# Two attention blocks on one core: the maxima's rows without TensorE, two projection groups moved into the loop, and one order for all loop steps

## The chip, the cores and the metric

The kernel runs on one core of a Trainium2 chip. The metric is the device time of one execution in microseconds (us). Before the change the median of 3 runs is 1849.92 us (1848.37 to 1851.09).

Five engines work side by side, each through its own instructions in program order: TensorE (PE, with its weight loads PEld), VectorE (DVE), ScalarE (ACT), GpSimd (POOL) and the DMA queue of SyncE (SP). They wait for each other through semaphores.

## The reference

Two attention blocks on 2048 rows of width 640, 32 heads of 20 columns each, both in float32. Block A is a dilated sliding window (8 keys per row), block B is full attention:

```python
q, k, v = x @ wqkv                       # per head 2048 x 20
scores = einsum("bhqd,bhkd->bhqk", q, k) * 20 ** -0.5
o = einsum("bhqk,bhkd->bhqd", softmax(scores), v)
out = o @ wo                             # A and B side by side
```

## The kernel before, in words

**Projections (0 to 442 us).** First Q, K and V of block A, then Q and K of block B, then V of block B. V of block B is made in 32 groups of 128 rows by 320 columns (lines 758 to 791): 15 matmuls into one of the four small PSUM banks `ps_st`, a copy by ScalarE into a tile `ve`, and a store to `vb_d` in DRAM one tick later.

**Block B, the loop (442 to 1805 us).** 8 head groups of 4 heads, 4 query blocks (`qc`) of 512 rows each, 16 key blocks of 128 rows each: 8 x 4 x 16 = 512 steps, numbered `i`, and 32 *units* of 16 steps (a unit is one head group and one query block). A step has three parts:

- `b_qk(i)`: the transposed scores of the step, 2 pairs of matmuls (the two of a pair work on different halves of the rows of the array), and 4 exponentials by ScalarE into tiles `e`.
- `b_pv(i - 2)`: the product with V, two steps later (`LAG`), 4 matmuls in the program and 8 in the trace. `hold` says over how many steps it is summed in PSUM: 2, so that ScalarE copies (`more`) and GpSimd adds (`braw`) once in two steps. Units 27 to 29 (`ALONE`) have `hold` 1.
- `b_max(i + 24)`: the plain scores of a step 24 later (`LEAD`), 2 pairs of matmuls into one of two wide PSUM tiles `ps_mx` each, and for each a maximum over 512 keys by VectorE (`mx<-ps_mx`). The softmax needs the row maximum before its exponential, so the maxima run 24 steps ahead of it.

**Maxima's rows.** At the end of a unit's 16 maxima, `max_rows` (line 560) makes one number per query of them and hands it to the score matmuls as two more rows of the tile `bq` (one rounded, one with the rest), against rows of -1 in `bk`. VectorE reduces `m4` to `m1` (128 x 16, `mx<-mx`); two ticks later `turn` is put into the list `rows`, which the loop takes up in its odd steps: TensorE transposes `m1` into a PSUM bank (`ps_st<-ident,mx`), ScalarE copies 16 x 128 of it (`mtr`), VectorE subtracts the copy from the bank for the rest, the bank is given back; one tick later one DMA stores 16 x 2 x 128 to `mdr` in DRAM, and one more tick later two DMAs load the rows into `bq` (`bq<-mdr`). In the loop, for unit u, the reduction comes at step 16u-7, the transpose at 16u-5, the store at 16u-4, the load at 16u-3; the unit's first score matmul is in step 16u.

**Steps 432 to 479** (units 27 to 29) go through `b_both` (line 632) in place of `b_qk` and `b_max`: score matmuls and maxima's matmuls alternate one by one, on opposite halves of the array, and the product with V comes last.

**The V groups and the maxima.** The first 24 steps of `b_max` have to come before the loop; one of them follows each V group from the 9th to the 32nd (`groups > 8`, line 780). The Q rows that they need are loaded after the first four V groups, four DMAs each.

**Other work in the loop.** Block A's attention is GpSimd's (`akv`, `al`, `ao`); its output projection comes as pieces of 15 matmuls (`ps_st<-ww,aot`) in some steps. The sum of the exponentials comes back through DRAM as a tile `sm`, of which VectorE takes the reciprocal (`sm<-sm`). `after(n, ...)` puts an instruction n ticks (steps) later; its engine's own order is the order in which these calls run. All transfers named here go through SP's queue, in order; each waits until the one eight places before it has landed.

Of the kernel before, what the change touches and what calls it, by code (L numbers as in the profile page):

```python
# [8 lines left out]
F32 = mybir.dt.float32  # L9
# [8 lines left out]
DH = 20  # L18
# [24 lines left out]
ALONE = range(27, 30)  # L43
# [16 lines left out]
def attention_pair(ctx, tc, xa, wqk_a, wv_a, wo_a, xb, wqk_b, wv_b, wo_b, oa, ob):  # L60
# [497 lines left out]
    rows = []  # L558
# [48 lines left out]
    mxt = {}  # L607

    def b_max(i):
# [4 lines left out]
        if sub == 0:  # L614
            mxt[u] = (sb.tile([128, 2, 8, 4], F32, tag="mx4", bufs=2, name="mx4"),
                      sb.tile([128, 16], F32, tag="mx1", bufs=2, name="mx1"))
# [14 lines left out]

    def b_both(i):

        u, kb = divmod(i, NKB)
        g, qc = divmod(u, NQC)
        q, k, v = stacks[g]
        P[i] = []
        i1 = i + LEAD
        u1, sub = divmod(i1, NKB)
        g1, qc1 = divmod(u1, NQC)  # L640
        q1, k1, _ = stacks[g1]
        if sub == 0:
            mxt[u1] = (sb.tile([128, 2, 8, 4], F32, tag="mx4", bufs=2, name="mx4"),
                       sb.tile([128, 16], F32, tag="mx1", bufs=2, name="mx1"))
        m4, m1 = mxt[u1]
        pq, ch = divmod(sub, 2)
        pl1, qb = divmod(pq, 4)
        for pl in range(2):
            e = sb.tile([128, 2, 512], F32, tag="p", bufs=PB, name="e")
            c = 2 * ch + pl  # L650
            w = wide()
            for r in range(2):
                rows = slice(r * HALF, r * HALF + BM)
                p = bank()
                pe.matmul(p, k[rows, pl, kb * 128:kb * 128 + 128], q[rows, qc, pl], start=True, stop=True)
                act.activation(e[:, r], p, AF.Exp, scale=SCALE)
                give(p)
                rows = slice((1 - r) * HALF, (1 - r) * HALF + BS)
                pe.matmul(w[:, 1 - r], q1[rows, qc1, pl1, qb * 128:qb * 128 + 128],
                          k1[rows, pl1, c * 512:(c + 1) * 512], start=True, stop=True)  # L660
            dve.tensor_reduce(m4[:, :, pq, c], w, AX.X, ALU.max)
            P[i].append(e)
        if sub == NKB - 1:
            max_rows(m4, m1, q1, qc1)
# [26 lines left out]
    def b_pv(i):  # L691
        u, kb = divmod(i, NKB)
        g, qc = divmod(u, NQC)
        hold = 1 if u in ALONE else 2
        n, part = divmod(kb, hold)
# [3 lines left out]
        for j in range(GH):  # L699
            pe.matmul(acc[32 * j:32 * j + 32, :], stacks[g][2][:, kb, j * VC:j * VC + 32], P[i][j % 2][:, j // 2],  # L700
                      start=(part == 0), stop=(part == hold - 1))
        del P[i]
        if part < hold - 1:
            return
# [53 lines left out]
    for n in (2, 3, 0, 1):  # L758
        for half in range(2):
            for s in range(4 * n, 4 * n + 4):  # L760
                p = bank()
                rows15(p, lambda xi, k: chunk(XB[n], xi, k)[:, s % 4 * 128:s % 4 * 128 + 128], WV[half])
                ve = ones[s % 4]
                act.copy(ve[:, :16 * VC].rearrange("p (h c) -> p h c", c=VC)[:, :, :DH],
                         p[:, :320].rearrange("p (h d) -> p h d", d=DH))
                give(p)
                c = 16 * VC + 11 * half
                after(1, sp.dma_start, vb_d[s * 128:(s + 1) * 128, half * 16 * VC:half * 16 * VC + c], ve[:, :c])
                tick()
                groups += 1  # L770
                if q_loads:
                    for _ in range(4):
                        q_loads.pop(0)()
                if groups == 1:
                    wait[0] = 5
                if groups in (8, 16):
                    XB[groups // 8 - 1], more = x_pieces(xb, groups // 8 - 1, gp)
                    for fn in more:
                        fn()
                if groups > 8:  # L780
                    for i in islice(steps, 1):
                        for _ in b_max(i):
                            pass
                    if rows:
                        rows.pop(0)()
                if groups > 16 and groups % 3 == 0 and groups != 21:
                    next(a_work, None)
                if groups in (26, 28):
                    v_piece(0, *((0, 4) if groups == 26 else (8, 16)))
# [4 lines left out]
    for h in range(2):  # L794
        w, more = wide_pieces(wo_a[h], gp)
        WO.append(w)
        loads += more
    assert next(steps, None) is None

    spare += [sb.tile([128, 2, 512], F32, tag="last0", bufs=2, name="more") for _ in range(2)]
# [14 lines left out]
    for i in range(NS + LAG):  # L817
# [16 lines left out]
        if i // NKB in ALONE and i + LEAD < NS:  # L834
            b_both(i)
            if rows and i % 2:
                rows.pop(0)()
            b_pv(i - LAG)
            if fill and i % 2 == 0:
                fill.pop(0)()  # L840
            elif i % 6 == 4 and not out_piece() and not left_a[0] and not WO_b:
                for h in range(2):
                    w, more = wide_pieces(wo_b[h], gp)
                    WO_b.append(w)
                    loads += more
            continue
        if i + LEAD >= NS:
# [3 lines left out]
            if rows and i % 2:  # L851
                rows.pop(0)()
# [8 lines left out]
        if rows and i % 2:  # L861
            rows.pop(0)()
        if i >= LAG:
            b_pv(i - LAG)
        next(qk, None)
        mx = b_max(i + LEAD)
        next(mx, None)
        if fill and i % 2 == 0:
            fill.pop(0)()
        elif i % 6 == 4 and not out_piece() and not left_a[0] and not WO_b:  # L870
            for h in range(2):
                w, more = wide_pieces(wo_b[h], gp)
                WO_b.append(w)
                loads += more
# [58 lines left out]
```

## Time and profile before

| | us |
|---|---|
| median of 3 runs | 1849.92 |
| the profiled execution's own time | 1849.53 |
| its span in the trace | 1847.8 |
| PE busy (matmuls) | 1805.9 (98%) |
| ScalarE busy | 1363.9 (74%) |
| VectorE busy | 1320.7 (71%) |
| GpSimd busy | 1233.1 (67%) |
| first score matmul of step 0 | 442.24 |
| first score matmul of step 432 / 480 | 1586.28 / 1710.36 |

The matmuls' ends are modelled and overlap, so a PE busy at 98% is not a PE at its limit. The times of steps are taken from the timeline: a step begins with its first score matmul (`ps_st<-bq,bk`). A row of the windows view has the stretch (us from the span's start), its length, then for PE, PEld, DVE, ACT and POOL the busy time and number of instructions, the granted clock of TensorE (1.00 is full), the DMA share and GB/s.

### The profile page before, as it was taken

Reading aid. Unit: us, or ns where it says so; the run is one execution under the profiler, and the core shown is the slowest. Engines: PE = TensorE matmul, PEld = TensorE weight load, DVE = VectorE, ACT = ScalarE, POOL = GpSimd, SP = SyncE. Lnnn points to the kernel's source line nnn. Section 1 sums busy time; section 2 is a strip of 40 time slices with the busy share of each in tenths; the row PEclk is TensorE's granted clock in tenths of the full one; section 3 lists DMA queues with packets and bytes.
Section 4 is the critical chain, followed back from the end, with each engine's and each line's share of the span. In section 5 each row is a group of like instructions: output and inputs, shape, how many; then the busy total and the mean of one; then the engine's idle time right before and its main releaser. Section 6 shows DMA issues by size and latency. Waiting matters only on the chain.

```text
span 1847.8 us, 30664 instructions
## 1 busy us (share of the span) xinstructions
PE 1805.9 (98%) x11243; PEld 970.8 (53%) x11243; DVE 1320.7 (71%) x1350; ACT 1363.9 (74%) x2653; POOL 1233.1 (67%) x1030
## 2 busy tenths in 40 slices
PE   9999999999999999999999999999999999999999
PEld 8888888886334333343343343433434434434568
DVE  3100332278998999988989989899898898899400
ACT  4222322224998999988989989899898898899891
POOL 0000075038999989989899999899998872387332
PEclk9999999999999999999999999999999999999999
DMA  6323686655543364346325533653373232021023
GB/s 224 110 96 109 203 299 236 223 168 179 156 138 106 99 181 122 100 127 176 105 96 151 160 99 101 167 144 115 96 208 103 76 102 75 18 70 49 28 70 112
DMA packets 188398, 240.23 MB, mean 130 GB/s; under 512 B 85340, under 2 KB 116700, under 8 KB 187256
## 3 DMA queue, kind: packets, MB, share of 16 engines
q1 hardware_dynamic: 187672, 237.62, 42.3%
q8 instruction: 88, 1.44, 0.3%
q10 hardware_dynamic: 576, 0.66, 0.1%
q14 instruction: 62, 0.51, 0.1%
HBM read 173.29 MB, written 64.91 MB: 129 GB/s over the span
## 4 chain that ended last, share of the span: by engine, by line
PE 58%; DVE 23%; DMA 5%; ACT 5%; POOL 5%; issue 2%; SPq 1%; POOLq 0%; DVEq 0%; ACTq 0%
PE ps_st L56 40%; DVE mx L56 22%; PE ps_mx L56 18%; ACT e L56 4%; POOL akv L56 3%; ACT more L56 1%; SPq L56 1%; POOL braw L56 1%; DMA aq<-qa_d 1%; DMA akv<-va_d 1%; DMA s_d<-braw 1%; DMA akv<-ka_d 1%; DMA tr_d<-turn 1%; DVE am L56 0%; DVE turn L56 0%
## 5 line engine op out<-in xcount | busy, mean ns | idle before, releaser
L56 DVE TENSOR_REDUCE mx<-ps_mx 128x2 f32<-128x1024 f32 x1024 | 1199.2, 1218 | 138.0 <-PE ps_mx L56 130.7
L56 ACT ACTIVATE e<-ps_st 128x512 f32<-128x512 f32 x2000 | 1063.0, 614 | 49.8 <-PE ps_st L56 23.3
L56 PE MATMUL ps_st<-e,vb 128*32 128x512 f32 x4096 | 544.6, 606 | 1.1 <-ACT e L56 0.6
L56 PE MATMUL ps_st<-bq,bk 62*128 62x512 f32 x2000 | 492.3, 453 | 0.5 <-ACT e L56 0.2
L56 PEld LDWEIGHTS ps_st<-bq,bk 62*128 62x128 f32 x2000 | 258.3, 184 | 431.6 <-ACT e L56 394.5
L56 PE MATMUL ps_mx<-bk,bq 60*128 60x512 f32 x2048 | 444.5, 443 | 34.0 <-DVE mx L56 19.7
L56 POOL TENSOR_TENSOR braw<-braw,more 128x512 f32<-128x512 f32 x248 | 318.8, 1285 | 194.4 <-ACT more L56 187.9
L56 POOL TENSOR_TENSOR akv<-akv,aq 128x1280 f32<-128x1280 f32 x64 | 188.4, 2943 | 237.2 <-DMA akv<-ka_d 237.2
L56 PEld LDWEIGHTS ps_mx<-bk,bq 60*128 60x128 f32 x2048 | 204.4, 185 | 188.4 <-DVE mx L56 175.7
L56 POOL TENSOR_TENSOR akv<-akv 128x640 f32<-128x640 f32 (+3 forms) x304 | 281.7, 927 | 23.8
L56 PEld LDWEIGHTS ps_st<-e,vb 128*32 128x32 f32 x4096 | 82.1, 108 | 153.5 <-ACT e L56 90.2
L56 ACT COPY more<-ps_st 128x512 f32<-128x512 f32 x248 | 149.9, 604 | 14.9 <-PE ps_st L56 7.6
L56 ACT COPY ro<-ps_st 128x320 f32<-128x320 f32 (+1 forms) x92 | 43.6, 474 | 155.6 <-PE ps_st L56 110.2
L56 POOL TENSOR_TENSOR akv<-akv,al 128x1280 f32<-128x1280 f32 x64 | 151.5, 2367 | 0.2
L56 PE MATMUL ps_st<-ww,xn 128*128 128x320 f32 x720 | 119.8, 314 | 0.0
L56 PEld LDWEIGHTS ps_st<-ww,xn 128*128 128x128 f32 x720 | 106.7, 188 | 19.8 <-ACT e L56 8.7
L56 POOL TENSOR_TENSOR xn<-stg,xn 128x512 fp32r<-128x512 f32 (+1 forms) x20 | 30.1, 1508 | 92.4 <-ACT xn L56 91.1
L56 DVE TENSOR_TENSOR wc<-stg,wc 128x480 fp32r<-128x480 f32 (+5 forms) x15 | 8.4, 559 | 101.9 <-ACT wc L56 101.9
L56 PE MATMUL ps_st<-ww,aot 128*128 128x320 f32 x480 | 78.8, 316 | 0.0
L56 POOL TENSOR_TENSOR ao<-ao,akv 128x640 f32<-128x640 f32 x48 | 74.9, 1560 | 3.8
L56 PEld LDWEIGHTS ps_st<-ww,aot 128*128 128x128 f32 x480 | 70.4, 188 | 12.2 <-ACT e L56 6.3
L56 ACT COPY ro<-ps_mx 128x480 f32<-128x480 f32 x32 | 18.0, 562 | 72.0 <-PE ps_mx L56 62.5
(84 smaller groups left out, 1308.1 us busy)
## 6 DMA issues: line engine op xcount, KB each, us to landing
akv<-ka_d SPq DMA_DIRECT2D x128, 320.0 KB
akv<-va_d SPq DMA_DIRECT2D x128, 320.0 KB
kb_d<-pr SPq DMA_DIRECT2D x20, 512.0 KB
qb_d<-pr SPq DMA_DIRECT2D x20, 512.0 KB
bk<-kb_d SPq DMA_DIRECT2D x16, 640.0 KB
bq<-qb_d SPq DMA_DIRECT2D x64, 160.0 KB
rb<-s_d SPq DMA_DIRECT2D x128, 64.0 KB
stg<-xb SPq DMA_DIRECT2D x12, 512.0 KB
```

The source lines that it names most:

```text
L56: return lambda *a, **k: self.tc.keep_in_program_order(op(*a, **k))
```

## The change

Three edits.

**1. Maxima's rows.** `m1` becomes one of two lasting 128 x 32 tiles, cleared once by GpSimd, of which the reduction fills 16 columns. VectorE transposes it in blocks of 32 x 32 right behind the reduction; one tick later GpSimd makes the rounded part (a copy, 128 x 32) and the rest (a subtraction, 128 x 32); two ticks after that four DMAs of 16 x 2 x 32 store them (pieces of 128 bytes where they had 512), and the load comes one tick later, at the same step as before. TensorE, ScalarE and the PSUM bank have no part in it any more.

**2. V's last two groups** move into steps 0 and 1 of the loop, between their two pairs of score matmuls, where a product with V would be in later steps. The maxima begin after the 7th group in place of the 9th. The second half of block A's output weights is loaded after them.

**3. Steps 432 to 479** are as all others; `ALONE` and `b_both` go.

```diff
-ALONE = range(27, 30)
...
     def max_rows(m4, m1, q, qc):
-        mt = sb.tile([16, 2, 128], F32R, tag="mtr", bufs=2, name="mtr")
+        mt = sb.tile([128, 3, 32], F32R, tag="mtr", bufs=2, name="mtr")
         md = dr.tile([2, GH * 512], F32, tag="mdr", bufs=4, name="mdr")
+        raw = mt[:, 0].bitcast(F32)
         def turn():
-            p = bank()
-            pe.transpose(p[:16, :128], m1, ident)
-            act.copy(mt[:, 0], p[:16, :128])
-            dve.tensor_tensor(mt[:, 1], p[:16, :128], mt[:, 0].bitcast(F32), ALU.subtract)
-            give(p)
-            after(1, sp.dma_start, md.rearrange("t (j c) -> j t c", c=128), mt.bitcast(F32))
-            after(2, load)
+            dve.transpose(raw, m1)
+        def parts():
+            gp.tensor_copy(mt[:, 1], raw)
+            gp.tensor_tensor(mt[:, 2], raw, mt[:, 1].bitcast(F32), ALU.subtract)
+        def store():
+            for b in range(4):
+                sp.dma_start(md.rearrange("t (j b c) -> b j t c", b=4, c=32)[b], mt[32 * b:32 * b + 16, 1:].bitcast(F32))
...
         t = odd(1)
-        after(t, dve.tensor_reduce, m1, m4.rearrange("p r a c -> p (r a) c"), AX.X, ALU.max)
-        after(t + 2, rows.append, turn)
+        after(t, dve.tensor_reduce, m1[:, :16], m4.rearrange("p r a c -> p (r a) c"), AX.X, ALU.max)
+        after(t, turn)
+        after(t + 1, parts)
+        after(t + 3, store)
+        after(t + 4, load)
...
-        hold = 1 if u in ALONE else 2
-        n, part = divmod(kb, hold)
+        n, part = divmod(kb, 2)
...
+    V_GROUPS = [(n, half, s) for n in (2, 3, 0, 1) for half in range(2) for s in range(4 * n, 4 * n + 4)]
+    v_late = V_GROUPS[-LAG:]
+    for n, half, s in V_GROUPS[:-LAG]:
+        v_group(n, half, s)
...
-                if groups > 8:
+        if groups > 6:
...
-        if i // NKB in ALONE and i + LEAD < NS:
-            b_both(i)
...
         if i >= LAG:
             b_pv(i - LAG)
+        else:
+            v_group(*v_late.pop(0))
+            if not v_late:
+                load_out(wo_a, WO, (1,))
```

**VectorE in the loop, around step 25 (unit 2's maxima end).** `mx<-ps_mx` are the maxima, `sm` the reciprocal of an earlier unit, `mtr` the tile of the rows. Before:

```order
L56 TENSOR_REDUCE mx_4248<-ps_mx 128x2 x2
L56 RECIPROCAL sm<-sm 128x16
L56 TENSOR_REDUCE mx_3713<-mx_3712 128x16
L56 TENSOR_REDUCE mx_4248<-ps_mx 128x2 x2
L56 STREAM_TRANSPOSE turn<-ao 128x128
L56 TENSOR_REDUCE mx_4248<-ps_mx 128x2 x2
L56 STREAM_TRANSPOSE turn<-ao 128x128
L56 TENSOR_TENSOR mtr<-ps_st,mtr 16x128
```

The same place in the changed program:

```order
L55 TENSOR_REDUCE mx_4253<-ps_mx 128x2 x2
L55 RECIPROCAL sm<-sm 128x16
L55 TENSOR_REDUCE mx_2553<-mx_3716 128x16
L55 STREAM_TRANSPOSE mtr<-mx_2553 128x32
L55 TENSOR_REDUCE mx_4253<-ps_mx 128x2 x2
L55 STREAM_TRANSPOSE turn<-ao 128x128
```

The subtraction two steps after the reduction is gone, and a transpose stands right behind the reduction and reads what it wrote.

**TensorE where V's groups end and the loop begins.** `ps_st<-ww,xn` and `ps_st<-ww,xl` are the 15 matmuls of a V group, `ps_mx<-bk,bq` the maxima's, `ps_st<-bq,bk` the scores', `ps_st<-e,vb` the product with V. Before, from the last V group to step 2:

```order
L56 MATMUL ps_st<-ww,xl 128x320 x3
L56 MATMUL ps_mx<-bk,bq 128x512 x4
L56 MATMUL ps_st<-bq,bk 128x512 x4
L56 MATMUL ps_mx<-bk,bq 128x512 x4
L56 MATMUL ps_st<-bq,bk 128x512 x4
L56 MATMUL ps_mx<-bk,bq 128x512 x4
L56 MATMUL ps_st<-bq,bk 128x512 x2
L56 MATMUL ps_st<-e,vb 32x512 x4
```

And in the changed program:

```order
L55 MATMUL ps_mx<-bk,bq 128x512 x4
L55 MATMUL ps_st<-bq,bk 128x512 x2
L55 MATMUL ps_st<-ww,xn 128x320 x12
L55 MATMUL ps_st<-ww,xl 128x320 x3
L55 MATMUL ps_st<-bq,bk 128x512 x2
L55 MATMUL ps_mx<-bk,bq 128x512 x4
L55 MATMUL ps_st<-bq,bk 128x512 x2
L55 MATMUL ps_st<-ww,xn 128x320 x12
L55 MATMUL ps_st<-ww,xl 128x320 x3
L55 MATMUL ps_st<-bq,bk 128x512 x2
L55 MATMUL ps_mx<-bk,bq 128x512 x4
```

Steps 0 and 1 now hold a V group each, between their pairs of score matmuls.

**TensorE at step 432.** Before, from step 431's second pair of scores on:

```order
L56 MATMUL ps_st<-bq,bk 128x512 x2
L56 MATMUL ps_mx<-bk,bq 128x512 x4
L56 MATMUL ps_st<-bq,bk 128x512
L56 MATMUL ps_mx<-bk,bq 128x512
L56 MATMUL ps_st<-bq,bk 128x512
L56 MATMUL ps_mx<-bk,bq 128x512
```

And in the changed program:

```order
L55 MATMUL ps_st<-bq,bk 128x512 x2
L55 MATMUL ps_mx<-bk,bq 128x512 x4
L55 MATMUL ps_st<-bq,bk 128x512 x2
L55 MATMUL ps_st<-e,vb 32x512 x4
L55 MATMUL ps_st<-bq,bk 128x512 x2
L55 MATMUL ps_mx<-bk,bq 128x512 x4
```

Two maxima's pairs no longer follow each other so closely there; a product with V stands between them again.

More of the change, by code (lines that the diff above doesn't have):

```diff
@@ L630, in b_max @@
             max_rows(m4, m1, q, qc)
[L632 to L664, printed above, removed]
     P = {}
@@ L757, in attention_pair @@
     groups = 0
[L758 to L779, printed above, removed]
-                if groups > 8:
[L781 to L789, printed above, removed]
@@ L860, in attention_pair @@
         next(qk, None)
-        if rows and i % 2:
-            rows.pop(0)()
         if i >= LAG:
             b_pv(i - LAG)
+        else:
+            v_group(*v_late.pop(0))
+            if not v_late:
+                load_out(wo_a, WO, (1,))
+                spare += [sb.tile([128, 2, 512], F32, tag="last0", bufs=2, name="more") for _ in range(2)]
         next(qk, None)
@@ L870, in attention_pair @@
         elif i % 6 == 4 and not out_piece() and not left_a[0] and not WO_b:
[L871 to L874, printed above, removed]
+            load_out(wo_b, WO_b)
         next(mx, None)
```

61 lines of the change are left out of this document (39 added, 22 removed).

## The prediction

> **What bounds the kernel now.** I read the page's shares and chain first, then the costliest groups.
>
> ```profile
> PE 1805.9 (98%) x11243; PEld 970.8 (53%) x11243; DVE 1320.7 (71%) x1350; ACT 1363.9 (74%) x2653; POOL 1233.1 (67%) x1030
> ...
> PE 58%; DVE 23%; DMA 5%; ACT 5%; POOL 5%; issue 2%; SPq 1%; POOLq 0%; DVEq 0%; ACTq 0%
> ...
> L56 DVE TENSOR_REDUCE mx<-ps_mx 128x2 f32<-128x1024 f32 x1024 | 1199.2, 1218 | 138.0 <-PE ps_mx L56 130.7
> ...
> L56 PEld LDWEIGHTS ps_mx<-bk,bq 60*128 60x128 f32 x2048 | 204.4, 185 | 188.4 <-DVE mx L56 175.7
> ```
>
> The chain is 58% TensorE and 23% VectorE, and the two wait for each other: VectorE 130.7 us for the maxima's matmuls, the weight loads of these 175.7 us for VectorE to empty a wide bank. So the loop has no single owner; a change has to be priced in whole steps. For that I cut the timeline at the first score matmul of chosen steps and asked for the busy times between the cuts; the columns behind the length are PE, PEld, DVE, ACT, POOL.
>
> ```profile
> 364.61:366.81 2.20, 2.20 (x18) 2.20 (x17) 0.00 (x0) 0.28 (x1) 0.00 (x0) 1.00 0.54 202
> 380.47:411.08 30.61, 30.61 (x193) 25.02 (x192) 24.09 (x21) 9.10 (x16) 12.93 (x7) 1.00 0.48 152
> 442.24:447.22 4.98, 2.93 (x18) 1.40 (x16) 4.98 (x7) 3.90 (x9) 0.58 (x3) 1.00 0.76 199
> 848.90:851.60 2.70, 0.77 (x6) 0.44 (x6) 2.70 (x5) 1.09 (x2) 2.70 (x2) 1.00 0.84 294
> 851.60:855.00 3.40, 3.40 (x15) 0.84 (x15) 2.65 (x4) 1.62 (x4) 3.24 (x3) 0.50 0.29 94
> 1057.10:1062.06 4.96, 4.84 (x34) 1.88 (x33) 4.96 (x7) 4.75 (x10) 4.72 (x4) 1.00 0.00 0
> 1062.06:1072.12 10.06, 9.76 (x69) 3.80 (x66) 9.49 (x10) 9.55 (x20) 9.67 (x10) 1.00 0.40 126
> 1126.10:1140.89 14.79, 14.40 (x98) 5.45 (x97) 14.04 (x13) 14.18 (x28) 13.93 (x16) 1.00 0.26 88
> 1579.35:1586.28 6.93, 6.92 (x49) 3.87 (x47) 4.66 (x5) 5.03 (x11) 1.28 (x1) 1.00 0.12 38
> 1586.28:1594.41 8.13, 6.82 (x35) 2.06 (x32) 6.43 (x6) 5.20 (x10) 1.27 (x1) 0.79 0.04 10
> 1586.28:1710.36 124.08, 122.06 (x789) 49.17 (x786) 115.58 (x107) 118.65 (x244) 83.40 (x73) 0.99 0.16 47
> ```
>
> Six plain steps (258 to 263) take 14.79 us, 4.93 a pair of steps. Two steps of which one has a piece of 15 output matmuls (430 and 431) take 6.93, so a piece costs 2.0. Times of steps come from this one execution, whose own time is 1849.53 us, 0.39 under the median of the runs shown; I sum against it.
>
> **V's last two groups.** A V group alone takes 2.20 us of TensorE; ten with maxima take 30.61, so 3.06 each, and the maxima cost 0.86. Steps 0 and 1 take 4.98, with TensorE busy for 2.93 of it and VectorE for all: there is room beside. Before: two groups with maxima and the two steps, 6.12 + 4.98 = 11.10. After: maxima behind the 7th and 8th group, 2 x 0.86 = 1.72; steps 0 and 1 held by TensorE, 2.93 + 2 x 2.20 = 7.33. That is 9.05, but the maxima now come earlier than the Q rows may be there:
>
> ```profile
> 355.90 3.61 SPq L56 DMA_DIRECT2D bq<-qb_d  x4
> ...
> 366.81 1.92 PE L56 MATMUL ps_st<-ww,xn 128*128 128x320 f32 x12
> ...
> 371.29 0.73 PE L56 MATMUL ps_mx<-bk,bq 60*128 60x512 f32 x4
> ```
> ```profile
> 368.27 0.27 SPq L56 DMA_DIRECT2D bq<-qb_d  x1
> ```
>
> The 8th group begins at 366.81, and there, at some 366.97, the first maxima would stand in the changed order; before, they start at 371.29. The last of the four Q loads that they need goes out at the end of the x4 row. The transfer issued at 368.27 is the eighth behind it, and the program lets that one go when it has landed. So TensorE waits about 1.3 us (none at best; 4.3 if the rows only just made 371.29). Term: 9.05 + 1.3 - 11.10 = **-0.75**, from -2.05 to +2.25. The pieces of V that steps 6 to 9 read are stored two steps later; they are asked for at step 3 as before, three steps ahead of their use, which I cost at nothing; without that cover a landing of some 2 us would show.
>
> What a wait of TensorE costs beyond itself: in the row from 851.60 the granted clock is 0.50 for 3.40 us, and in the 2.70 us before, TensorE was busy for 0.77. Half a clock for 3.40 us loses 1.7; the wait above could bring that too, which stays inside the bounds. The Trainium skill (TensorE: Matmul & The Clock Gate, part 1, "What's actually happening") has the clock halve only after a whole idle window of about 3.4 us; by that rule a wait of 1.3 us would never cost the 1.7 and the term stays -0.75. The row disagrees in part: the engine was not idle for that long.
>
> **Maxima's rows.** Removed and, as the nearest rows for what is added:
>
> ```profile
> L56 ACT CAST mtr<-ps_st x32: 238/238/276, 427.3 to 1745.8; 16x128 fp32r<-16x128 f32 x32
> L56 DVE TENSOR_TENSOR mtr<-ps_st,mtr x32: 235/269/279, 429.2 to 1746.1; 16x128 fp32r<-16x128 f32 x32
> ...
>   PEld ps_st L56: 20.3, 29
> ```
> ```profile
> L56 PE MATMUL ps_st<-ident,mx x32: 276/277/383, 427.0 to 1742.7; 128*16 128x128 f32 x32
> ```
> ```profile
> L56 DVE STREAM_TRANSPOSE turn<-ao 128x128 f32<-128x128 f32 x80 | 23.6, 295 | 0.0
> ...
> L56 DVE TENSOR_REDUCE mx<-mx 128x16 f32<-128x64 f32 x32 | 5.4, 169 | 0.1
> ...
> L56 POOL TENSOR_TENSOR am<-am 128x32 f32<-128x32 f32 x16 | 4.0, 253 | 1.3
> ```
>
> The transpose on TensorE lasts 277 ns, and weight loads wait 20.3 us in 29 waits (0.7 each) for the bank that VectorE and ScalarE empty. Most of it hides: the four steps from 1062.06, with one transpose in them, take 10.06 against 2 x 4.93, so **0.20** a unit. That is what can be won, 27 times in the loop's plain order (units 1 to 27): 5.4.
>
> Against it stands VectorE's transpose. A quarter of the 128 columns of `turn` (295 ns), and a small reduction beside it (169 ns): I take 0.2, and 0.08 for its wait on the reduction, 0.28 in all (0.17 to 0.4). It comes in the steps where the reciprocal and the reduction already stand: 1057.10 to 1062.06, with VectorE busy 4.96 of 4.96. They take 4.96 and not much more than 4.93, so what stood there found room, and used it up. The next four steps have 10.06 - 9.49 = 0.57 free, and 0.27 more since the subtraction goes; TensorE, at 9.76 with its transpose, can catch up a part. Between nothing and all of 0.28 I take a third, 0.1. Net 0.1 a unit won: **-2.7**, from -5.4 to 27 x 0.08 = +2.2. GpSimd's two instructions are some 0.5 us in 40 us (253 ns for the subtraction's shape); it has no part in the chain worth this, and the rows are due only steps later (below). Unit 0's transpose lies among V's groups and unit 31's in the loop's end: 0.28 each at the least, 0.7 at the most: **-0.5** (0 to -1.4).
>
> **Steps 432 to 479.** Before: 124.08 us. After: 24 pairs at 4.93, 118.3, one piece of output matmuls (step 436) 2.0, and three units' rows at 0.2 with what is left of them; 120.9. The difference, **-3.1**, is found whole in one place: steps 432 and 433 take 8.13 us, 3.2 over a pair, at a clock of 0.79. There the old order puts the maxima of step 432 straight behind two pairs of maxima of step 431, right after a piece of 15, and TensorE waits for both wide banks. With a product with V between them, as in steps 430 and 431 (6.93, nothing lost), I see no such wait. If the stall came from the piece itself and stays: 0. If the pairs are as in the best stretches: -4.
>
> **Sum.** -0.75 - 2.7 - 0.5 - 3.1 = -7.05; 1849.53 - 7.05 = 1842.5.
>
> **Rivals.**
>
> *VectorE becomes the bound in the rows' steps.* For it speaks the 4.96 of 4.96. Then all of 0.28 shows in each unit and the rows' term is +2.2: 1849.53 - 0.75 + 2.2 - 0.5 - 3.1 = 1847.4, no change by measure. Against it: 0.84 us free just behind.
>
> *All hides, and a chance stall goes.* VectorE's transpose costs nothing (-5.4), no wait for Q (-2.05), and the stall at 848.90 to 855.00, which began with VectorE waiting for a transfer, does not come back (some 3): 1849.53 - 5.4 - 2.05 - 0.5 - 3.1 - 3 = 1835.5.
>
> *The rows come late: slower.* They now go through GpSimd's queue and four DMAs in place of one, and the score matmul of step 16u waits for them. Units 10 and 22 are tight in this trace, unit 11 is ordinary:
>
> ```profile
> 861.80 0.53 SPq L56 DMA_DIRECT2D bq<-mdr  x2
> ...
> 899.44 0.32 SPq L56 DMA_DIRECT2D mdr<-mtr  x1
> 900.88 0.52 SPq L56 DMA_DIRECT2D bq<-mdr  x2
> ...
> 1368.79 0.52 SPq L56 DMA_DIRECT2D bq<-mdr  x2
> ```
> ```profile
> 865.41 0.41 PE L56 MATMUL ps_st<-bq,bk 62*128 62x512 f32 x2
> ...
> 909.42 0.41 PE L56 MATMUL ps_st<-bq,bk 62*128 62x512 f32 x2
> ...
> 1372.90 0.40 PE L56 MATMUL ps_st<-bq,bk 62*128 62x512 f32 x2
> ```
> ```profile
> 1331.41 1.41 SPq L56 DMA_DIRECT2D ot_b<-braw  x4
> ```
>
> In unit 11 the load goes out 1.44 us after the store, which is what a small transfer takes to land. Unit 10's loads go out at 861.80 and 0.3 later, land near 863.5, and are needed at 865.41: 1.9 to spare. Unit 22 has 2.4, unit 11 over 6. Three more issues, at the 1.41 us that four take (`ot_b`), are 1.05 later, and unit 10 keeps 0.8. Both tight units lie in the steps in which a head group's K and Q are loaded; one unit in four does. If all eight of these wait alike, a delay of D costs 8 x (D - 2): at 5 us 24, which gives 1842.5 + 24 = 1866.5. It turns to slower than before, by more than 3.7, from a D of about 3.4 us. What speaks against it: I count 1.05.
>
> The pieces stored are 128 bytes where they were 512. The Trainium skill (DMA: Bandwidth & Descriptors, Specifications) gives 512 bytes as the least for full rate, with a read-modify-write below it; by that the four stores land later than the one did, which adds to this rival. No row here times a store by its size.
>
> **How the numbers follow.** The forecast, with the terms near what I took (1838 to 1846), 0.55; VectorE as the bound 0.22; all hides 0.13; rows late 0.10. What a measurement of this kernel can tell from no change is some 0.2%, 3.7 us: faster is under 1846.2. Faster: 0.13 + 0.55 less a little at its upper edge, 0.67; same 0.23; slower 0.10. The range 1835 to 1851 takes in the first three cases and the bounds of the terms, and leaves out the late rows and the best of the best case.
>
> **What would show it.** Right: no `ident,mx` group in the loop; steps 432 to 479 in about 121 us with no clock of 0.5 at 432; V's groups with a first maximum at about 368.4 and steps 0 and 1 in some 7.3 us; four steps around a unit's rows in about 9.9 to 10.0. Wrong: score matmuls of steps 16u waiting for `bq<-mdr`; VectorE full in the two steps of the transpose with the pair over 5.1; a clock of 0.5 after the wait for Q; or a new stall where the reciprocal waits for its transfer.

## The result and the profile after

The changed kernel takes **1845.63 us**, the median of 13 runs (1842.64 to 1851.18); the kernel before, run beside it, 1849.69 (13 runs, 1846.0 to 1853.25). The ratio is 0.9988, with a 95% interval from 0.9979 to 0.9997: a little faster, by 0.6 to 3.9 us in 1850. The profiled execution has a span of 1846.1 us and its own time is 1847.92, so it is one of the slower ones; against the profile before it is 1.6 us shorter. One execution of a kernel further down (2317.31 us, at a granted clock of 0.65) and one of the kernel before beside it (5467.55 us) lie far off all others, and the ratios and that kernel's median leave them out.

The page of the kernel after, its shares, its chain and the two groups that carried the argument before:

```profile
PE 1797.0 (97%) x11211; PEld 961.3 (52%) x11211; DVE 1319.3 (71%) x1350; ACT 1352.8 (73%) x2597; POOL 1214.2 (66%) x1072
...
PE 7%; DVE 1%; issue 0%; ACT 0%
...
L55 DVE TENSOR_REDUCE mx<-ps_mx 128x2 f32<-128x1024 f32 x1024 | 1196.8, 1217 | 139.0 <-PE ps_mx L55 136.7
...
L55 PEld LDWEIGHTS ps_mx<-bk,bq 60*128 60x128 f32 x2048 | 193.0, 185 | 208.5 <-DVE mx L55 197.7
```

32 matmuls fewer on TensorE are the transposes. The chain is followed back only over the last 8% of the span this time, so its shares say nothing against the 58% and 23% of before. What can be compared are the waits between TensorE and VectorE: 136.7 us (130.7 before) and 197.7 (175.7). TensorE does less and waits for VectorE more.

The same cuts in the timeline as before, at the first score matmuls of the same steps (a row: stretch, length, busy time of PE, PEld, DVE, ACT, POOL, clock, DMA share, GB/s):

```profile
440.47:447.58 7.11, 7.11 (x48) 5.84 (x46) 5.16 (x7) 4.19 (x10) 6.32 (x6) 1.00 0.69 212
482.99:531.05 48.06, 45.21 (x286) 19.92 (x288) 38.29 (x42) 37.98 (x74) 46.17 (x41) 0.96 0.62 164
1058.09:1063.06 4.97, 4.89 (x34) 1.99 (x33) 4.91 (x7) 4.77 (x10) 4.89 (x3) 1.00 0.09 34
1063.06:1072.91 9.85, 9.39 (x66) 3.36 (x65) 9.39 (x10) 9.36 (x19) 9.37 (x12) 1.00 0.38 108
1357.05:1365.42 8.37, 6.37 (x35) 2.10 (x33) 5.06 (x8) 4.84 (x10) 7.26 (x7) 0.80 0.48 160
1361.60:1365.00 3.40, 3.40 (x16) 0.99 (x18) 2.03 (x2) 1.65 (x3) 3.32 (x3) 0.50 0.15 50
1488.02:1493.39 5.37, 4.83 (x35) 1.55 (x33) 5.30 (x8) 4.88 (x11) 4.38 (x6) 1.00 0.26 85
1588.54:1593.60 5.06, 4.93 (x35) 1.92 (x33) 4.82 (x5) 4.86 (x10) 1.29 (x2) 1.00 0.07 16
1588.54:1709.16 120.62, 117.00 (x787) 45.00 (x784) 113.39 (x106) 113.82 (x218) 56.20 (x57) 1.00 0.16 48
```

Three things came as forecast: steps 0 and 1 in 7.11 us, the pair with VectorE's transpose unchanged at 4.97 and the four steps behind it at 9.85 (10.06 before), steps 432 and 433 at 5.06 in place of 8.13. The second row, steps 16 to 31, and the fifth, steps 346 and 347, did not. Cutting both timelines at the same steps says where the 1.6 us come from:

| stretch | before | after | difference |
|---|---|---|---|
| first V matmul to step 2 | 95.78 | 95.64 | -0.14 |
| steps 2 to 15 | 34.72 | 35.41 | +0.69 |
| steps 16 to 31 | 44.82 | 48.06 | +3.25 |
| steps 32 to 143 | 295.67 | 294.76 | -0.91 |
| steps 144 to 159 | 42.98 | 40.82 | -2.16 |
| steps 160 to 335 | 467.07 | 465.38 | -1.69 |
| steps 336 to 351 | 40.42 | 43.31 | +2.89 |
| steps 352 to 431 | 213.38 | 213.22 | -0.17 |
| steps 432 to 479 | 124.08 | 120.62 | -3.46 |
| step 480 to the end | 137.39 | 136.98 | -0.42 |

The differences sum to -2.1; all before V's first matmul took 0.50 longer, which gives -1.6.

**Steps 16 to 31.** The timeline of TensorE has one wait of 1.88 us there, on ScalarE's exponentials:

```profile
499.36 0.49 PE L55 MATMUL ps_st<-bq,bk 62*128 62x512 f32 x1 [1.88 <-ACT e L55]
```

ScalarE had stood still itself. In its timeline, before and after, the exponential of block A (`al`) waits for GpSimd, and the exponentials of the loop are queued behind it:

```profile
495.59 0.42 ACT L56 ACTIVATE al<-al 128x256 f32<-128x256 f32 x1 [0.69 <-POOL al L56]
```
```profile
498.40 0.42 ACT L55 ACTIVATE al<-al 128x256 f32<-128x256 f32 x1 [2.42 <-POOL al L55]
```

And GpSimd's timeline, before and after: the piece of block A's output weights that it last waited for, and the subtraction that ScalarE needs.

```profile
450.23 0.72 POOL L56 CAST ww<-stg 128x640 fp32r<-128x640 f32 x1 [0.71 <-DMA stg<-wo_a]
...
494.82 0.74 POOL L56 TENSOR_TENSOR al<-al,am 128x256 f32<-128x256 f32 x1
```
```profile
452.64 0.72 POOL L55 CAST ww<-stg 128x640 fp32r<-128x640 f32 x1 [1.51 <-DMA stg<-wo_a]
...
497.66 0.72 POOL L55 TENSOR_TENSOR al<-al,am 128x256 f32<-128x256 f32 x1
```

Between the two rows GpSimd works without a break, 44.59 us before and 45.02 after: the 0.43 more are the rounded part and the rest of a unit's rows. The piece comes 2.41 later; these pieces are asked for one in each odd step of the loop, and steps 0 and 1 are 2.13 longer now. So the subtraction is 2.84 later, while step 21 begins only 1.08 later (495.61 against 494.53), and ScalarE's wait grows from 0.69 to 2.42. Behind TensorE's wait the clock is at 0.50 for 3.4 us, from 501.5 on. The order of the same queue makes unit 1's rows late: their loads go out 1.5 us ahead of step 16 (3.7 before), and TensorE waits 0.75 us for them.

**Steps 346 and 347.** VectorE's timeline after:

```profile
1358.55 0.25 DVE L55 RECIPROCAL sm<-sm 128x16 f32<-128x16 f32 x1 [1.90 <-DMA sm<-s_d]
```

The maxima are queued behind this reciprocal; TensorE waits 1.36 and 0.63 us for them, and from 1361.6 the clock is at 0.50. It is the stall that stood at steps 154 and 155 before.

### The profile page after: what moved, and what is told of

Same layout as the page of the kernel before. It is cut to its first block, busy times and chain, and to the rows that moved or that the text cites. A ratio compares the mean times of both kernels' runs of the same rounds, so it can differ in the third digit from the quotient of the medians.

```text
span 1846.1 us, 30585 instructions
## 1 busy us (share of the span) xinstructions
PE 1797.0 (97%) x11211; PEld 961.3 (52%) x11211; DVE 1319.3 (71%) x1350; ACT 1352.8 (73%) x2597; POOL 1214.2 (66%) x1072
## 5 line engine op out<-in xcount | busy, mean ns | idle before, releaser
L55 DVE TENSOR_REDUCE mx<-ps_mx 128x2 f32<-128x1024 f32 x1024 | 1196.8, 1217 | 139.0 <-PE ps_mx L55 136.7
L55 PE MATMUL ps_st<-bq,bk 62*128 62x512 f32 x2000 | 470.8, 455 | 2.6 <-ACT e L55 2.6
L55 PEld LDWEIGHTS ps_st<-bq,bk 62*128 62x128 f32 x2000 | 246.9, 184 | 425.2 <-ACT e L55 411.7
L55 PE MATMUL ps_mx<-bk,bq 60*128 60x512 f32 x2048 | 422.3, 442 | 39.9 <-DVE mx L55 23.4
L55 POOL TENSOR_TENSOR braw<-braw,more 128x512 f32<-128x512 f32 x224 | 287.5, 1284 | 182.7 <-ACT more L55 176.9
L55 PEld LDWEIGHTS ps_mx<-bk,bq 60*128 60x128 f32 x2048 | 193.0, 185 | 208.5 <-DVE mx L55 197.7
L55 ACT COPY more<-ps_st 128x512 f32<-128x512 f32 x224 | 132.4, 591 | 12.6 <-PE ps_st L55 5.8
L55 DVE TENSOR_TENSOR xl<-stg,xl 128x512 fp32r<-128x512 f32 x12 | 8.3, 688 | 95.9 <-ACT xl L55 95.9
```

The source lines that it names most:

```text
L55: return lambda *a, **k: self.tc.keep_in_program_order(op(*a, **k))
```

## The experiments

All ratios are to the kernel before, run beside each on the same chip (its medians there: 1848.67 to 1849.36).

**Edit 1 alone** (the rows, on the kernel before):

```diff
-            pe.transpose(p[:16, :128], m1, ident)
...
+            dve.transpose(raw, m1)
```

> The maxima's rows alone (first edit), V's groups and steps 432 to 479 as before. Theory: the transpose on TensorE with its held PSUM bank cost some 0.2 us a unit and VectorE's transpose costs nothing, so the four steps from 16u+10 take about 9.85 us (10.06 before), the two steps ahead of them stay at 4.9 to 5.0, and the time falls by 27 x 0.2 = 5.4 us in the plain steps and about 1 us in steps 432 to 479; step 432 keeps its stall of 3 us. Rival: the gain of the whole change came from elsewhere and VectorE's transpose takes back what TensorE's gave: the pair ahead grows by 0.2 and the time stays within 1 us. Beside that, stalls of 1 to 4 us with half a clock may come or go where the reciprocal waits for its transfer.

Measured: 1847.57, ratio 0.9997 [0.9988, 1.0006].

```profile
1059.59:1064.57 4.98, 4.90 (x35) 2.00 (x33) 4.94 (x7) 4.77 (x10) 4.67 (x5) 1.00 0.00 0
1064.57:1074.43 9.86, 9.40 (x68) 3.38 (x65) 9.38 (x10) 9.37 (x19) 9.54 (x11) 1.00 0.38 109
1587.65:1594.29 6.64, 5.42 (x35) 1.87 (x33) 6.40 (x6) 5.19 (x10) 1.26 (x1) 1.00 0.05 12
```

The steps behind the rows have their 0.2 as in the whole change. The medians do not tell the edit from no change, since a part is lost again: ScalarE's wait at step 21 is 1.56 us here, with half a clock behind it (steps 16 to 31 take 47.22), though V's groups are where they were: GpSimd's subtraction ends 0.58 later than before, counted from V's first matmul, and step 21 begins 0.29 sooner. The last row says something of edit 3: the old order at step 432 costs 1.6 us over 5.06 without half a clock, and 3.1 with it.

**Edit 2 alone** (V's last two groups, on the kernel before):

```diff
+    for n, half, s in V_GROUPS[:-LAG]:
...
+        if groups > 6:
...
+            v_group(*v_late.pop(0))
```

> V's last two groups and the maxima's earlier start alone (second edit). Theory: the first maxima wait about 1.6 us for the Q rows, step 2 begins 0.4 us later than before, GpSimd comes out of the loop's first steps later, and ScalarE's exponential of block A waits for it in step 21: some 2 to 4 us are lost there, with half a clock; in all 1 to 4 us slower than before. Rival: the stall at step 21 needs GpSimd's two added instructions a unit (first edit) and is not there; then the edit is worth nothing, within 1 us.

Measured: 1851.67, ratio 1.0016 [1.0007, 1.0024]. Slower, by 1.3 to 4.4 us. ScalarE at step 21:

```profile
496.99 0.42 ACT L56 ACTIVATE al<-al 128x256 f32<-128x256 f32 x1 [2.38 <-POOL al L56]
```

Half a clock follows from 498.1, and steps 16 to 31 take 47.69 against 44.82. At step 2 it is 0.67 us ahead (95.11 from V's first matmul in place of 95.78), as good as the -0.75 forecast; so it loses not where its matmuls stand but 20 steps later.

**Edit 3 alone** (one order for all steps, on the kernel before):

```diff
-ALONE = range(27, 30)
+ALONE = range(0)
```

> Steps 432 to 479 in the order of all others, alone (third edit). Theory: the stall at steps 432 and 433 (8.13 us before) goes, the pair takes about 5.0, and steps 432 to 479 take about 121.5 us with the transposes on TensorE still in (124.08 before): 2.5 us faster. Rival: the stall belongs to the piece of output matmuls of step 430 and stays: 124 us and no change.

Measured: 1848.41, ratio 0.9995 [0.9986, 1.0003].

```profile
1587.94:1593.01 5.07, 4.94 (x36) 1.92 (x33) 4.83 (x5) 4.87 (x10) 1.30 (x2) 1.00 0.07 16
1587.94:1709.17 121.23, 118.11 (x788) 46.44 (x787) 113.88 (x106) 114.39 (x221) 54.98 (x51) 1.00 0.16 48
```

The stall is gone and the stretch is 2.85 shorter. In this profile 1.9 of it are lost in steps 2 and 3, at a clock of 0.50 from 446.5 for 6.8 us, and a half clock at step 347 stands where before one stood at step 155. The 2.85 us so rest on the stretch in the profile; the medians do not tell this edit from no change.

Taken alone, the three edits measure -1.7, +2.4 and -0.9 us between the medians, each good to some 1.7 us. That is -0.2 in all, where together they make -4.1. A good part of the gap is the stall at step 21: it stands in the run of edit 1 and in that of edit 2 (steps 16 to 31 take 2.40 and 2.87 more than before) and only once in the whole (3.25).

**No wait for Q** (the kernel after, maxima one group later, the last two steps of maxima behind one group):

```diff
-        if groups > 6:
-            for i in islice(steps, 1):
+        if groups > 7:
+            for i in islice(steps, 2 if groups == 30 else 1):
```

> The changed kernel, with the maxima from the 8th V group on and two of them behind the last: only the wait for the Q rows is taken away. Theory: TensorE loses no time at its first maxima (1.6 us in the changed kernel), and the loop's step 2 begins about 1.3 us earlier (446.3 in place of 447.6). The stall at step 21 stays or grows, since GpSimd's backlog does not depend on it. Rival: the wait is made good by later slack and step 2 begins where it did.

Measured: 1847.29, ratio 0.9995 [0.9985, 1.0006]. TensorE's timeline at the first maxima, after and here:

```profile
368.61 0.47 PE L55 MATMUL ps_mx<-bk,bq 60*128 60x512 f32 x1 [1.14 <-DMA bq<-qb_d]
369.55 0.69 PE L55 MATMUL ps_mx<-bk,bq 60*128 60x512 f32 x3 [0.47 <-DMA bq<-qb_d]
```
```profile
369.35 0.73 PE L55 MATMUL ps_mx<-bk,bq 60*128 60x512 f32 x4
```

The wait, 1.61 us, is gone; step 2 comes 95.36 us behind V's first matmul (95.64 after), so only 0.3 came back. The run below with VectorE's transpose twice happens to have no wait for Q but 0.11, and its step 2 comes at 94.10: the wait costs 1.5, about itself, and two steps of maxima behind one group cost 1.3 of that again. ScalarE's wait at step 21 (2.05 us here) stays, as it must if Q is not its cause. The time is no better than that of the kernel after.

**Half of block A's output weights earlier** (the kernel after; the first half is loaded and split by GpSimd behind V's 28th to 30th group, not in the loop):

```diff
+        if groups == 28:
+            load_out(wo_a, WO, (0,))
+        if groups >= 28:
+            loads.pop(0)()
...
-    load_out(wo_a, WO, (0,))
```

> The changed kernel, with the first half of block A's output weights loaded and split during V's groups 28 to 30 in place of the loop's first odd steps. Theory: GpSimd was 2 to 3 us late in the loop's first 22 steps, which made unit 1's rows late (TensorE waits 0.75 us at step 16) and ScalarE's exponential of block A wait 2.4 us in step 21; GpSimd then comes there 3 us earlier, both waits go, and steps 16 to 31 take about 44.5 us in place of 48.06: 3 to 4 us faster than the changed kernel. Rival: GpSimd is full from 425 us on whatever the order of its work, the exponential comes as late, and steps 16 to 31 stay near 48.

Measured: 1843.05, ratio 0.9970 [0.9958, 0.9981], with this in ScalarE's timeline:

```profile
496.77 0.42 ACT L55 ACTIVATE al<-al 128x256 f32<-128x256 f32 x1 [1.15 <-POOL al L55]
```

No half clock follows, and steps 16 to 31 take 45.36 (48.06 after). The wait is halved, not gone.

**The same, split by ScalarE and VectorE**, which takes some 6 us from GpSimd:

```diff
-            w, more = wide_pieces(src[h], gp)
+            w, more = wide_pieces(src[h], second)
...
-            load_out(wo_a, WO, (0,))
+            load_out(wo_a, WO, (0,), None)
```

> As e5_weights, but the halves of block A's output weights that come early are split by ScalarE and VectorE during V's last groups, and not by GpSimd, which so has about 6 us less to do in front of step 21. Theory: GpSimd's load between V and step 21 is what makes ScalarE's exponential of block A late. Then its wait (1152 ns in e5_weights, 2416 in the kernel after) falls under 0.3 us, unit 1's stored rows come in time, and steps 16 to 31 take 44.0 to 44.6 (e5_weights 45.36); 1 to 1.5 us less than e5_weights, if V's matmuls do not wait for ScalarE and VectorE (at most 0.3 us expected). Rival: the place of V's moved groups itself makes GpSimd's chain late and the weights have no more to give: the wait stays at about 1 us and the blocks too, and V takes up to 1 us more; 1843 to 1844.

Measured: 1843.57, ratio 0.9966 [0.9954, 0.9979].

```profile
494.61 0.42 ACT L55 ACTIVATE al<-al 128x256 f32<-128x256 f32 x1
```

ScalarE no longer waits, steps 16 to 31 take 44.03, less than before the change, and unit 1's rows wait for nothing. So GpSimd's load ahead of step 21 is the cause, which both runs together show: less of it, less wait; 6 us less, none. The median is no lower than that of the run before, so the 1.3 us in these steps do not show in the time of the whole. What else is left in its runs (1839.66 to 1844.29) the one profile, that of the quickest, does not show; with the edit below that is called "both of these" they lie between 1837.49 and 1839.68.

**The reciprocal and all behind it two steps later** (the kernel after):

```diff
-        t = odd(t + 3)
+        t = odd(t + 5)
```

> The changed kernel, with the reciprocal and all that follows it two steps later. Theory: the stalls at steps 346 and 347 (8.36 us in place of 4.95), and the smaller ones at 154, come from VectorE standing at a reciprocal whose transfer has not landed; with two steps more none is left and no half clock follows there: about 3 to 5 us faster than the changed kernel. Rival: the transfers are late by more than two steps, or VectorE's stalls have another cause: within 1 us.

Measured: 1885.11, ratio 1.0197 [1.0182, 1.0213]. Neither theory. The outputs' stores moved as well, and a tile that they hold came free too late; ScalarE's copy in its timeline:

```profile
838.51 0.59 ACT L55 COPY braw<-ps_st 128x512 f32<-128x512 f32 x1 [5.53 <-DMA ot_b<-braw]
```

There are two such tiles, and every fourth unit lacked one; TensorE waits 4.96 us behind it, with half a clock after that. Steps 346 and 347 were quick, but the run can't be read for that.

**The reciprocal, its store and its broadcast alone two steps later**, the multiplication one step later and the outputs' stores where they were (on the kernel with the weights earlier):

```diff
-        after(t, dve.reciprocal, sm, sm)
-        after(t + 1, sp.dma_start, s_d[1].rearrange("j (p c) -> j p c", c=16), sm)
-        after(t + 2, bcast)
-        after(t + 4, pool, raw, raw, rb, ALU.mult)
+        after(t + 2, dve.reciprocal, sm, sm)
+        after(t + 3, sp.dma_start, s_d[1].rearrange("j (p c) -> j p c", c=16), sm)
+        after(t + 4, bcast)
+        after(t + 5, pool, raw, raw, rb, ALU.mult)
```

> The weights' part of e5_weights, and beside it the reciprocal of the sums, its store and its broadcast two steps later, with the copies, raw stores and output multiplications where they were. Theory: the stalls at steps 154/155 and 346/347, of which each profile so far shows one or none, are VectorE's reciprocal waiting in its queue for the sums' transfer, and behind it TensorE; with two steps more they are gone from every unit, the clock is not at 0.5 anywhere from step 32 to step 480 and every block of 16 steps from 32 on stays within 0.8 us of its lowest time in any profile; 2 to 3 us less than e5_weights where that has such a stall (1843.05), so about 1840.5 to 1841.5. Rival: the broadcast now lands after GpSimd wants it for the outputs, GpSimd is late instead and the rows with it: outputs' multiplications wait over 0.5 us each unit, and the time is e5_weights' or more.

Measured: **1838.43**, ratio 0.9944 [0.9931, 0.9957]. Steps 154 and 155, and 346 and 347:

```profile
846.97:851.87 4.90, 4.74 (x36) 1.78 (x33) 4.90 (x6) 4.74 (x10) 4.82 (x5) 1.00 0.57 179
1352.50:1357.41 4.91, 4.76 (x35) 1.79 (x33) 4.81 (x6) 4.76 (x10) 4.75 (x7) 1.00 0.93 256
```

Plain pairs, where the kernel after has 6.26 and 8.37; the clock is at full through the whole loop. The gain over the run with the weights alone is 4.6 us between the medians, where I expected 2 to 3; in the two profiles 3.7 of it are these two pairs (6.09 and 7.46 with the weights alone) and 1.0 a shorter wait for Q. The theory holds: every block from step 32 on is within 0.8 us of its lowest time in any profile (the widest is steps 144 to 159, 40.24 against 39.57), and no reciprocal in the loop waits before step 499.

**Both of these**:

```diff
+        after(t + 2, dve.reciprocal, sm, sm)
...
+            load_out(wo_a, WO, (0,), None)
```

> Both of e10_reciprocal2 and e11_split. Theory: the two gains add, since they lie at different places: about 1839.5 to 1841, the least of all kernels here. Rival: the one or the other is not there, and the time is that of e5_weights (1843.05) within 1 us.

Measured: 1838.47, ratio 0.9945 [0.9933, 0.9957]; the runs lie between 1837.49 and 1839.68. Steps 16 to 31 take 43.88 (45.24 with the reciprocal alone), so the second gain is there, but step 2 comes 95.95 behind V's first matmul where it came 94.60, and the wait for Q, longer in this execution, has taken it back:

```profile
368.38 0.47 PE L55 MATMUL ps_mx<-bk,bq 60*128 60x512 f32 x1 [1.29 <-DMA bq<-qb_d]
369.48 0.70 PE L55 MATMUL ps_mx<-bk,bq 60*128 60x512 f32 x3 [0.63 <-DMA bq<-qb_d]
370.11 2.03 PE L55 MATMUL ps_st<-ww,xn 128*128 128x320 f32 x12
```

Whether the two differ at all their medians don't tell. They are the best versions here, 10 us under the kernel before.

**The later reciprocal in the kernel before**, with nothing else:

> The kernel before with one edit: the reciprocal of the sums, its store and its broadcast two steps later, the multiplication one step later. Theory: the chance stalls where VectorE's reciprocal waits for the sums' transfer belong to the kernel before as well, and make up most of the spread of its runs (1846 to 1853). Without them the clock is not at 0.5 between steps 32 and 431, the block from step 144 takes 40.8 at the most (42.98 in the profile before), and the median is 1846 to 1847 with its runs within 3 us of each other (one place with a clock of 0.5, at step 432, stays). Rival: the reciprocal's later place collides in the kernel before with what VectorE has to do for the rows two steps behind the reduction (the subtraction from the bank), so that nothing or something is lost: 1849 to 1853, and the four steps behind each unit's rows over 10.1.

Measured: 1846.26, ratio 0.9981 [0.9972, 0.9989], 12 runs from 1844.82 to 1847.59. Steps 144 to 159 take 39.87 (42.98 before), and the stall at step 432 stays:

```profile
847.64:853.03 5.39, 5.12 (x36) 1.75 (x33) 5.39 (x8) 5.08 (x12) 5.23 (x5) 1.00 0.84 244
1584.08:1592.19 8.11, 6.82 (x35) 2.06 (x33) 6.41 (x6) 5.20 (x10) 1.26 (x1) 0.79 0.04 10
```

So these stalls belong to the kernel before too, at 3 us in the median, and much of the spread of its runs is theirs (2.8 us from the lowest to the highest, 7.3 in the 17 runs of the kernel before beside it). One expectation missed: a half clock stands at 446.7, in the loop's first steps.

**VectorE's transpose twice** (the kernel after; the second writes the same again):

```diff
             dve.transpose(raw, m1)
+            dve.transpose(raw, m1)
```

> The changed kernel with VectorE's transpose of the maxima done twice, one behind the other: the suspected cost doubled. Theory: VectorE has room there for both and nothing moves, the pair of steps ahead stays at 4.95 and the four behind at 9.85. Rival: the first transpose used up VectorE's room, so each further 0.2 us shows in full: pairs of 5.15, and 30 x 0.2 = 6 us slower than the changed kernel.

Measured: 1851.92, ratio 1.0016 [1.0007, 1.0025]. The pair with the transposes and the four steps behind it:

```profile
1060.82:1065.80 4.98, 4.90 (x35) 2.00 (x33) 4.94 (x7) 4.78 (x10) 4.59 (x7) 1.00 0.00 0
1065.80:1075.89 10.09, 9.38 (x66) 3.33 (x65) 9.59 (x11) 9.35 (x19) 9.85 (x9) 1.00 0.40 110
```

The pair itself doesn't move; the 0.21 us of the second transpose come out in the steps behind, in full. Most other units lose as much; in five the second costs nothing either. So the room was there for one, and in most units the one took it.

**A transpose on TensorE as well** (the kernel after; into one of the four small banks, read by no one):

```diff
+        def idle_turn():
+            p = bank()
+            pe.transpose(p[:32, :128], m1, ident)
+            give(p)
...
+        after(t + 2, idle_turn)
```

> The changed kernel with a transpose of the maxima on TensorE added into a PSUM bank that nobody reads, two steps after the reduction as before the change: TensorE's instruction is back, the bank is free at once. Theory: the 0.2 us a unit lay in TensorE's own instruction (about 0.28 us with its weight load), and come back: the four steps take about 10.05 us, 27 x 0.2 = 5 us slower than the changed kernel. Rival: they lay in the bank held until ScalarE and VectorE had read it, and the four steps stay at 9.85 to 9.9.

Measured: 1859.55, ratio 1.0057 [1.0044, 1.0070].

```profile
1064.34:1069.31 4.97, 4.89 (x35) 1.98 (x33) 4.92 (x7) 4.77 (x10) 4.74 (x4) 1.00 0.00 0
1069.31:1079.56 10.25, 9.77 (x69) 3.67 (x66) 9.38 (x10) 9.36 (x19) 9.85 (x12) 1.00 0.37 110
```

0.40 more in the four steps (10.25 against 9.85), twice what the theory had, with no ScalarE and no VectorE reading the bank. So TensorE's instruction and its turn in the banks are enough to cost time, without readers. It stands ahead of a step's first scores here, not where the old one stood, so the 0.40 is not the old one's price, which was 0.21; how much of that the readers had is not shown.

## Why the prediction was right, and where it was wrong

The time, 1845.63, lies 3 us over the 1842.5 predicted: of the 7 us forecast 4 came. Term by term, in the two profiled executions:

**V's groups: predicted -0.75 (to +2.25), measured -0.14 at step 2, and then a loss of some 3 further on.** The parts were near: steps 0 and 1 at 7.11 (7.33), the wait for Q 1.61 (1.3; it lies between 0.11 and 1.92 in the nine profiles that have it, so the near hit is luck). Some half a us more went where I had no term, most of it into the first group with maxima: 5.06 us, where 3.06 and the wait make 4.67. The step that failed is that GpSimd stands in no term: "it has no part in the chain worth this", said of edit 1's two instructions, and for edit 2 not weighed at all. I had followed V's own instructions, and not the weights whose pieces are asked for in the same steps, which I had just found to become 2 us longer. From the piece that it waits for to step 21 GpSimd has no pause in which to catch up, and ScalarE waits for it at the head of its own queue. Edit 2 alone shows the loss with the rows left as they were; edit 1 alone shows that a few tenths on GpSimd are enough to begin it; taking 6 us from GpSimd makes it vanish. Edit 2 also has a gain that these two profiles don't show: of the four with V's groups at their old place, where TensorE is busy for 2.93 of the 4.98 us of steps 0 and 1, two have half a clock from 446.5 or 446.7 on (the runs of edit 3 and of the later reciprocal); of the ten with the groups in these steps none has.

**Rows: predicted 0.1 a unit, measured 0.12.** In the 23 units without a stall (from step 32 to 431 without the blocks of 144 and 336) the blocks of 16 steps are 2.77 shorter, and it is edit 1: alone it takes 2.71 off the same blocks, where edit 2 adds 0.55 and edit 3 takes off 0.03. The size is right, and the reason only on average. In most units all of the 0.2 is kept, since the transpose on VectorE (0.21 us, where I took 0.2 and a wait) hides in full; there I gave back 0.1 too much. In the blocks of units 2, 3, 10, 22 and 24, in which the rows of the next unit are made, nothing is kept or something lost, up to 0.34 (0.14 of that are late rows, below). Unit 24 is the plainest; before, two steps behind the reduction:

```profile
1485.67:1490.81 5.14, 4.86 (x35) 1.75 (x34) 5.04 (x8) 4.84 (x11) 3.79 (x4) 1.00 0.33 116
```

After, the row at 1488.02 above: 5.37, with VectorE busy for 5.30 of it. There the rival "VectorE becomes the bound" holds, and so it does in units 3, 10 and 22 (5.56, 5.57 and 5.18 us with VectorE busy for 5.50, 5.49 and 5.18); in unit 2 VectorE has room in the pair that grew, and the cause is open.

**Late rows: the slower rival's mechanism is there, at 0.9 us** (0.75 at step 16 and 0.14 in unit 10). I counted a delay of 1.05. In unit 10 the loads go out 1.5 us ahead of the step where they had 3.3, a delay of 1.8, and the unit's first two steps are 0.14 longer; the queue's view says why:

```profile
859.31 3.56 SPq L55 DMA_DIRECT2D mdr<-mtr  x4
...
864.81 0.53 SPq L55 DMA_DIRECT2D bq<-mdr  x2
```

The four stores stand in the queue for 3.56 us, not the 1.41 that I took from another group of four (in most units they take 1.7 to 1.8). Unit 22 kept 4.4, and all others but unit 1 have 3.6 or more. The size of the pieces shows no cost: the quickest load goes out 1.45 us behind the last store, as it did with pieces of 512 bytes (1.43). The Trainium skill (DMA: Bandwidth & Descriptors, Specifications) has a read-modify-write below 512 bytes; if there is one here, these landings don't show it.

**Steps 432 to 479: predicted 120.9, measured 120.62.** The stall at the entry is gone as said. The prediction names the clock of 0.79 there and does not say what it means: half of the stall's 3.1 us was half a clock. It costs 1.6 in the run of edit 1, where the clock stayed whole.

**Units 0 and 31: predicted -0.5.** All behind step 480, unit 31's rows with it, is 0.42 shorter; unit 0's lie among V's groups and can't be told from the rest there. So the term is not shown by itself.

**The stall that I took for chance.** The rival had it that the stall at 848.90 does not come back, with 0.13. It is no chance: in all ten kernels that have the reciprocal in its old place, VectorE waits for the sums' transfer at step 154 and at step 346, between 0.51 and 2.79 us. What changes from run to run is how long, and whether half a clock follows. I read one of the two from the profile before and priced it as luck; its twin at step 346 was there as well (0.51 us). In the profile after the two together cost 0.73 more than before. Two steps of lead for one transfer are worth 3.1 us in the kernel before, nearly what the three edits are together (4.1 between the medians).

So the sum stayed inside the range because it has terms of both signs: -3.5 for the order, -2.8 for the rows, and +3.9 in steps 2 to 31 for a delay on an engine that I had left out. The first two were reckoned; that the third was no larger is luck, since no term stood for it.

## What to carry to other kernels

An engine that is busy two thirds of the time can still have stretches of 45 us without a pause, and what makes it late there is paid 20 steps later, on another engine: when instructions are moved, follow each queue to the next place where it had waited, and see that it still does. A stall that shows once in a profile, with an in-order engine waiting for a transfer, is to be looked for at the same place in every unit and in other runs before it is called chance; giving it more steps of lead can be worth as much as the change at hand (3.1 and 4.6 us here, where the three edits bring 4.1). And a move that takes an operation off the critical engine is worth what the engine taking it has free in those very steps, once: the second transpose found nothing in most units.

## What the hardware showed beside

Half a clock follows short waits of TensorE, and not each time. Of the twenty waits for the sums in ten kernels six were followed by 3.4 us at 0.50; the shortest of them had VectorE waiting 1.03 us, and 2.24 us passed without. It also came where TensorE was never idle for longer than 1.1 us: in the run with the idle transpose on TensorE, behind the wait for Q.

```profile
368.17 0.46 PE L55 MATMUL ps_mx<-bk,bq 60*128 60x512 f32 x1 [1.07 <-DMA bq<-qb_d]
369.11 0.89 PE L55 MATMUL ps_mx<-bk,bq 60*128 60x512 f32 x3 [0.48 <-DMA bq<-qb_d]
369.93 3.34 PE L55 MATMUL ps_st<-ww,xn 128*128 128x320 f32 x12
```

Twelve matmuls take 3.34 us here, from a clock of 0.50 between 369.5 and 372.9; the same twelve take 2.03 in the run with both edits, behind a longer wait (1.29 and 0.63).

The traces say more of when. In every profile with several half clocks these begin whole multiples of 3.413 us apart (before at 851.63 and 1588.91, 216 of them; after at 501.45 and 1361.61, 252) and last one such window or two. So the clock goes by windows of 3.41 us, which lie differently in each execution. All 23 half clocks between V's first group and 1800 us came behind a window in which TensorE was busy for 0.70 of the time or less. The wait for Q in the run with the idle transpose lies in one window, with TensorE busy for 1.86 us of it:

```profile
366.05:369.46 3.41, 1.86 (x12) 1.26 (x10) 0.00 (x0) 0.43 (x1) 0.00 (x0) 1.00 0.52 164
```

In the run with both edits it falls across two, with 2.14 in the first and 2.76 in the second:

```profile
364.95:368.36 3.41, 2.14 (x15) 1.89 (x14) 0.00 (x0) 0.43 (x1) 0.00 (x0) 1.00 0.58 151
```

The busy time alone does not decide it: 13 windows under 0.70 passed without half a clock, one of them with 1.83 us of 3.41 (the run with the idle transpose, from 1366.15). What decides there is open. The Trainium skill (TensorE: Matmul & The Clock Gate, part 1, "What's actually happening") has the clock drop after a whole idle window of some 3.4 us, and lets the windows run freely, so that the moment falls differently in each run. The second half fits what these runs show; the first does not, since in this run no wait ahead of the half clock was longer than 1.07 us.
